# Linformer attention and a maxout feed-forward on one core: V projections through a doubled F, and one K/V projection moved by a slot

## The chip, the cores and the metric

The kernel runs on one core of a Trainium2 chip. The metric is the device time of one execution in microseconds, as a median of several runs. PE is the matrix engine (PEld its weight loads), DVE the vector engine, ACT the scalar engine, POOL the GpSimd engine and SP the queue of the sync engine.

## The reference

There are 8 batches of 8 heads, with 1024 positions and a head size of 64; E and F map the 1024 positions to 64.

```python
k_proj = np.einsum('ks,bhsd->bhkd', E, k)
v_proj = np.einsum('ks,bhsd->bhkd', F, v)
scores = (1 / np.sqrt(64)) * np.matmul(q, k_proj.transpose(0, 1, 3, 2))
attn = softmax(scores, axis=-1)
a = np.matmul(attn, v_proj)                    # (8, 8, 1024, 64)
x = a.transpose(0, 2, 1, 3).reshape(8192, 512)
h = np.maximum(np.maximum(x @ w1, x @ w2), x @ w3)   # 768 wide
out = h @ w_out                                # (8192, 512)
```

## The kernel before

The work is a pipeline over batches. While the feed-forward of batch b runs on PE, the attention of batch b+1 is laid between its groups of matmuls. A batch has two chunks of 512 rows. A chunk's layer 1 is 18 groups (`l1`, L212: six column tiles by three weights, four matmuls of 128x512 each, L215), and its down projection is four row blocks (`down`, L224, six matmuls each, L240). Layer 1 and down share a ring of four PSUM banks; the attention uses banks 4 to 7.

The order is written by hand. In the main loop every group of `l1` and every `down` ends a slot (`tick`, L560), and `at(slot, f, ...)` (L501) names what is emitted after which slot. Each engine executes its instructions in the order in which they are emitted. For batch 1 the list stands at L504 to L518: the K/V projection `kv` (L120) at slot 22, four Q transposes on DVE (`q_flip`, L103), the loads of batch 2 (`load_behind_turn`, L91) behind the transposed K projection, scores from slot 28 on. `kv` uses 16 matmuls (E on K at L123, F on V at L125, into the two halves of bank 4), two casts on ACT, two copies on DVE and a DMA transpose on SP's queue (L133) into `kpT`, which the scores (L145) read.

Batch 0 has its own opening, before the loop, since nothing is there yet that could hide its loads. E and F are loaded, cast and transposed by PE into `eT` and `fT` (L394 to L402; ACT evicts F). The loads of K, V and w1 to w3 and half of Q are issued from POOL, L370 to L384; the loads of w_out (L467) and those of batch 1 (L468 to L470) follow on the same queue. K and V of batch 0 are projected in pairs of heads. `v_proj0(g, bank)` (L282) takes 8 slices of 128 positions; for each it issues two matmuls with a 128x64 slice of F as weights and 64 columns of one head of V, one for each half of the output partitions; one DVE copy (L287) takes 128x64 into `vp2`. `half(g, u)` (L263) says which partitions a head of a pair gets: it swaps them for odd pairs. Between the steps stand warm-up matmuls (`warmup`, L350) on zeroes, that feed nothing.

The part around the change is emitted as follows: the projections of pairs 0 and 1, `av0(., 0)` (the products of probabilities and V for heads 0 to 3, L463), their normalisation on DVE (`norm0`, L309), the projection of pair 2 into bank 3 (L481), one warm-up matmul, the first slice of w1 over six column tiles (`w1_ct(0)`, L445, which writes bank 3 last), the projection of pair 3 into bank 7 (L484), three tiles of the second slice, then `av0(., 1)` for heads 4 to 7, and the remaining slices of w1.

In the last chunk of the kernel (c = 15), `down` (L226) splits row blocks 2 and 3 into two halves of 256 columns each, evicted by DVE and ACT and written out from the queues of SP and ACT. The other row blocks are evicted by ACT as a whole.

Of the kernel before, what the change touches and what calls it, by code (L numbers as in the profile page):

```python
# [10 lines left out]
BF16 = mybir.dt.bfloat16  # L11
# [5 lines left out]
def kernel(ctx: ExitStack, tc: tile.TileContext, q, k, v, E, F, w1, w2, w3, w_out, out):  # L17
    nc = tc.nc
    B, H, S, D = q.shape
    KP = E.shape[0]  # L20
    P = 128
    SI = S // P
# [9 lines left out]
    def T(shape, dt, name):  # L32
        return sb.tile(shape, dt, name=name)

    ps = pp.tile([P, 8, 512], FP32, name="ps")
# [5 lines left out]
    sel = T([P, 4, P], BF16, "sel")  # L41
    kp_0 = T([P, 2, 2, NPAIR, KP], BF16, "kp_0")
    eT = T([P, SI, KP], BF16, "eT")
    fT = T([P, SI, KP], BF16, "fT")
    w_sb = [T([P, NCT, DF], BF16, f"w{i}_sb") for i in range(3)]
    wo_sb = T([P, NJT, DO], BF16, "wo_sb")

# [2 lines left out]
    v_t = [T([P, H, SI, D], BF16, f"v_t{i}") for i in range(NB)]  # L50
# [4 lines left out]
    vp2 = [T([P, NPAIR, 2, D // 2], BF16, f"vp2_{i}") for i in range(3)]  # L55
# [5 lines left out]
    h1s = [T([P, 512], FP32, f"h1s{i}") for i in range(2)]  # L61
# [53 lines left out]
    HEAD = (0, 1, 2, 3, 5, 4, 7, 6)  # L115
# [107 lines left out]

    def down(b, ch, c, tt):  # L224
        o = o_acc[c % 2]
        if c == 2 * B - 1 and tt > 1:  # L226

            n = DO // 2
            for x in range(2):
                tmp = h1s[x] if tt == 3 else o[:, 2, x * n:(x + 1) * n]  # L230
                bank = fbank()
                for jt in range(NJT):
                    nc.tensor.matmul(out=ps[:, bank, :n], lhsT=hT[c % 2][:, jt, tt * P:(tt + 1) * P],  # L233
                                     rhs=wo_sb[:, jt, x * n:(x + 1) * n], start=(jt == 0), stop=(jt == NJT - 1))
                (nc.scalar.copy if x else nc.vector.tensor_copy)(out=tmp[:, :n], in_=ps[:, bank, :n])
                (nc.scalar if x else nc.sync).dma_start(out=out_v[b, ch][:, tt, x * n:(x + 1) * n], in_=tmp[:, :n])
            return
        bank = fbank()
        for jt in range(NJT):
            nc.tensor.matmul(out=ps[:, bank, :], lhsT=hT[c % 2][:, jt, tt * P:(tt + 1) * P],  # L240
                             rhs=wo_sb[:, jt, :], start=(jt == 0), stop=(jt == NJT - 1))
        nc.scalar.copy(out=o[:, tt, :], in_=ps[:, bank, :])  # L242
        if c == 2 * B - 1:
            nc.sync.dma_start(out=out_v[b, ch][:, tt, :], in_=o[:, tt, :])
        elif tt % 2 == 1:
            dst = out_v[b, ch] if b else out_0[ch]
            put = lambda: nc.gpsimd.dma_start(out=dst[:, tt - 1:tt + 1, :], in_=o[:, tt - 1:tt + 1, :])  # L247
            held.append(put) if c == 1 else put()
# [14 lines left out]
    def half(g, u):  # L263
        x = u ^ (g % 2)
        return slice(x * KP, (x + 1) * KP)
# [16 lines left out]
    def v_proj0(g, bank):  # L282
        for si in range(SI):
            for u in range(2):
                nc.tensor.matmul(out=ps[half(g, u), bank, g * D:(g + 1) * D], lhsT=fT[:, si, :],
                                 rhs=v_t[0][:, HEAD[2 * g + u], si, :], start=(si == 0), stop=(si == SI - 1))
        nc.vector.tensor_copy(out=vp2[0][:, g], in_=ps[:, bank, g * D:(g + 1) * D].rearrange("p (dd f) -> p f dd", f=2))  # L287

    def scores0(ch, g, bank):
        for u in range(2):  # L290
# [59 lines left out]
    def warmup(n, bank):  # L350
        for _ in range(n):
            nc.tensor.matmul(out=ps[:, bank, :], lhsT=warm[:, 0:P], rhs=warm, start=True, stop=True)
# [25 lines left out]
    for wt, w in zip(w_sb[1:], (w2, w3)):  # L378
        for hh in range(2):
            if wt is w_sb[2] and hh:  # L380
                nc.gpsimd.dma_start(out=q_1[:, 0:4], in_=qv_[1][:, 0:4])
            nc.gpsimd.dma_start(out=wt[:, 2 * hh:2 * hh + 2, :],
                                in_=w[hh * 256:(hh + 1) * 256].rearrange("(r f) n -> r f n", f=2))
# [10 lines left out]
    for y, dst in enumerate((eT, fT)):  # L394
        for si in range(SI):
            for x in range(2):
                nc.tensor.matmul(out=ps[x * D:(x + 1) * D, y, si * KP:(si + 1) * KP], lhsT=ef_b[:, y, si::SI],
                                 rhs=ident[:, x::2], start=True, stop=True)
        if y:
            for g in (0, 1):  # L400
                nc.scalar.copy(out=q_0[:, :, 2 * g, :], in_=q_st[:, HEAD[2 * g]])
        (nc.scalar.copy if y else nc.vector.tensor_copy)(out=dst.rearrange("p si k -> p (si k)"), in_=ps[:, y, :])  # L402

    def q_turn0(g):
        for n in range(4):
# [4 lines left out]
    def q_cast0(g):  # L410
        if g > 1:
            nc.scalar.copy(out=q_0[:, :, 2 * g, :], in_=q_st[:, HEAD[2 * g]])
        nc.vector.tensor_copy(out=q_0[:, :, 2 * g + 1, :], in_=q_st[:, HEAD[2 * g + 1]])

    SB = (0, 1, 4, 5)
    for g in range(NPAIR):
        q_cast0(g)
    warmup(1, 3)
    q_turn0(0)
    q_turn0(1)  # L420
# [57 lines left out]
    av0(1, 0)  # L478
    norm0(0, 0, 6, (0,))
    norm0(0, 1, 7, (0,))  # L480
    v_proj0(2, 3)  # L481
    warmup(1, 2)
    w1_ct(0)
    v_proj0(3, 7)  # L484
    w1_ct(1, range(3))
    av0(0, 1)
    av0(1, 1)
# [9 lines left out]
    for b in range(B):  # L497
        n = b + 1
        groups = []

        def at(slot, f, *args):  # L501
            groups.append((slot, lambda: f(*args)))

        if b == 0:  # L504
            at(8, q_up0, slice(4, 8))
            at(22, kv, 1)
            at(24, load_behind_turn, 2, "kvq")
            for g, x in enumerate((23, 24, 26, 27)):
                at(x, q_flip, 1, g)
            at(28, scores, 1, 0)  # L510
            at(31, scores, 1, 1)
            at(34, sums, 1)
            at(34, log, 1)
            at(34, recip, 0)
            at(35, recip, 1)
            at(36, av3, 1)
            at(37, norm, 1, 1, 0, AB)
            at(38, norm, 1, 0, 1, AB + 2)  # L518
        elif b == 1:
            at(2, kv, 2)  # L520
            for g in range(4):
                at(4 + g, q_flip, 2, g)
            at(9, load_behind_turn, 3, "kvq")
            at(10, scores, 2, 0)
            at(13, scores, 2, 1)
            at(16, sums, 2, 1)
            at(16, log, 1)
            at(17, recip, 0)
            at(19, recip, 1)
            at(24, load, 4, k, k_t)  # L530
            at(24, load, 4, v, v_t)
            at(25, av3, 2)
            at(26, norm, 2, 1, 0, AB)
            at(28, norm, 2, 0, 1, AB + 2)
            at(30, kv, 3)
            for g in range(4):
                at(32 + 2 * g, q_flip, 3, g)
        elif n < B:
            if b + 2 < B:
                at(3, lambda: kv(b + 2, fbank()))  # L540
            at(3, scores, n, 0)
            at(8, scores, n, 1)
            if b + 3 < B:
                at(11, load_behind_turn, b + 3, "qkv", 4 if b == 2 else None)
            at(14, sums, n, b)
            at(14, log, 1)
            at(15, recip, 0)
            at(17, recip, 1)
            at(26, av3, n)
            at(27, norm, n, 1, 0, AB)  # L550
            at(29, norm, n, 0, 1, AB + 2)
            if b + 2 < B:
                for g in range(4):
                    at(33 + 2 * g, q_flip, b + 2, g)
        else:
            at(5, av1, b)
        slot = 0
        gi = 0

        def tick():  # L560
            nonlocal slot, gi
            slot += 1
            while gi < len(groups) and groups[gi][0] <= slot:
                groups[gi][1]()
                gi += 1

        for ch in range(2):
            c = 2 * b + ch
            if c == 0:
                for part in ((1, range(6), (6, 7, 0, 1, 4, 5)), (2, range(3), (2, 3, 0), lambda: q_up0(slice(0, 4))),  # L570
                             (2, range(3, 6), (1, 2, 3), scores_up0)):
                    for _ in l1_first(*part):
                        tick()
                ring[:] = [0, 1, 2, 3]
                for x in range(2):
                    if x:
                        av_up0()
                    for tt in range(4):
                        down_half(tt, x)
                        if x:  # L580
                            tick()
                        elif tt == 0:
                            sums0(1, 4)
                continue
            for s in range(18):
                l1(b, ch, c, s // 3, s % 3)
                tick()
                if pend and s in (2, 5, 8, 11):
                    pend.pop(0)()
                    tick()  # L590
            pend = [lambda tt=tt, b=b, ch=ch, c=c: down(b, ch, c, tt) for tt in range(4)]
        if b == 0:
            while pend:
                pend.pop(0)()
                tick()
# [32 lines left out]
```

## Time and profile before

| | |
|---|---|
| median of 3 runs | 395.44 us (395.0 to 395.99) |
| the profiled execution | 394.96 us |
| its span, from the first to the last instruction | 393.1 us |
| PE busy | 387.7 us of the span |
| DVE, ACT, POOL busy | 202.5, 162.1, 67.0 us |
| DMA over the span | 123 GB/s mean; 205 GB/s in most of the first 50 us |

Times below are from the start of the span. A line of a timeline gives the start and the length of a run of like instructions, then engine, line, operation, tiles and count. Square brackets hold the idle time of the engine before it and what ended that.

### The profile page before, as it was taken

The page shows a single profiled execution, that of the slowest core. Times are in us where ns is not written, and L with a number is a line of the kernel's source. Part 1 is how long each engine was busy: PE and PEld are TensorE (multiplying, and loading weights), DVE is VectorE, ACT ScalarE, POOL GpSimd, SP SyncE. Part 2 cuts the span into 40 slices and gives each one's busy share as a digit, 9 for nine tenths or more (in the row PEclk, how much of TensorE's full clock was granted, in tenths as well). Part 3 has the DMA queues.
Part 4 walks back from the last instruction along what each step waited for, and adds up shares of the span by engine and source line. Part 5 has one row for each costly group of instructions (what it writes and reads, how often), then busy time and mean ns, then how long its engine had stood idle before and what let it go on. Part 6 is the DMA issues. An engine that isn't in the chain of part 4 may idle for free.

```text
span 393.1 us, 6707 instructions
## 1 busy us (share of the span) xinstructions
PE 387.7 (99%) x2768; PEld 173.2 (44%) x2768; DVE 202.5 (52%) x303; ACT 162.1 (41%) x248; POOL 67.0 (17%) x110
## 2 busy tenths in 40 slices
PE   8999999999999999999999999999999999999996
PEld 4444444444444444444444444444444444444443
DVE  3447565755663566345753357524664446453342
ACT  4413347374326622454224732266134542222221
POOL 7442132062004300050000600000010000000000
PEclk9999999999999999999999999999999999999999
DMA  8999989899974995169511992131011111111023
GB/s 221 206 210 204 205 173 203 135 208 206 206 160 86 201 205 179 24 123 206 157 53 28 172 212 101 53 82 53 2 58 50 54 55 54 55 45 63 0 106 107
DMA packets 41453, 48.39 MB, mean 123 GB/s; under 512 B 9168, under 2 KB 36560, under 8 KB 41424
## 3 DMA queue, kind: packets, MB, share of 16 engines
q0 software_dynamic: 31792, 43.52, 54.1%
q1 hardware_dynamic: 8656, 3.41, 4.8%
q10 hardware_dynamic: 976, 1.05, 0.8%
q8 instruction: 21, 0.34, 0.3%
q14 instruction: 8, 0.07, 0.0%
HBM read 57.15 MB, written 16.78 MB: 188 GB/s over the span
## 4 chain that ended last, share of the span: by engine, by line
PE 92%; DMA 6%; ACT 1%; POOL 0%; issue 0%; POOLq 0%
PE ps L215 59%; PE ps L240 19%; PE ps L123 3%; PE ps L159 3%; DMA w_sb<-in_moe_w_dram 3%; PE ps L456 2%; PE ps L145 2%; DMA k_t<-in_k_dram 2%; PE ps L254 1%; DMA kpT<-kp 1%; PE ps L447 1%; PE ps L233 1%; ACT pT L339 1%; PE ps L272 0%; POOL k_t L367 0%
## 5 line engine op out<-in xcount | busy, mean ns | idle before, releaser
L215 PE MATMUL ps<-xT,w_sb 128*128 128x512 bf16 x1080 | 244.3, 379 | 0.0
L215 PEld LDWEIGHTS <-w_sb 128*128 128x128 bf16 x1080 | 103.8, 98 | 129.7 <-issue 8.0
L220 DVE TENSOR_TENSOR m<-ps,h1s 128x512 f32<-128x512 f32 x90 | 62.0, 689 | 131.5 <-PE ps L215 98.4
L240 PE MATMUL ps<-wo_sb,hT 128*128 128x512 bf16 x348 | 84.2, 379 | 0.0
L218 ACT COPY h1s<-ps 128x512 f32<-128x512 f32 x90 | 52.9, 588 | 71.9 <-PE ps L215 71.7
L242 ACT COPY o_acc<-ps 128x512 f32<-128x512 f32 x58 | 34.0, 586 | 99.9 <-PE ps L240 99.9
L222 DVE TENSOR_TENSOR hT<-ps,m 128x512 bf16<-128x512 f32 x90 | 62.0, 689 | 8.1
L247 POOL DMA_DIRECT2D out_dram<-o_acc x28 | 15.2, 542 | 253.4 <-ACT o_acc L242 246.6
L240 PEld LDWEIGHTS <-hT 128*128 128x128 bf16 x348 | 33.4, 98 | 41.5 <-issue 2.3
L179 DVE TENSOR_TENSOR xT<-ps,rinv 128x1024 bf16<-128x1024 f32 x28 | 33.4, 1217 | 11.2 <-PE ps L159 11.2
L150 ACT ACTIVATE pT<-ps 128x1024 bf16<-128x1024 f32 x28 | 27.1, 1021 | 5.3 <-PE ps L145 4.9
L105 DVE STREAM_TRANSPOSE qT<-q_t 128x512 f32<-128x512 f32 x28 | 18.5, 686 | 0.0
L89 POOL DMA_DIRECT2D v_t<-in_v_dram x21 | 15.3, 753 | 8.4 <-PE ps L215 3.0
L170 ACT ACTIVATE lns<-ps 128x1024 f32<-128x1024 f32 x14 | 13.6, 1023 | 3.9 <-PE ps L159 3.9
L173 ACT ACTIVATE rinv<-lns 128x1024 f32<-128x1024 f32 x14 | 14.9, 1061 | 0.0
L125 PE MATMUL ps<-v_t,fT 128*64 128x512 bf16 x56 | 13.4, 382 | 0.0
L123 PE MATMUL ps<-k_t,eT 128*64 128x512 bf16 x56 | 13.4, 382 | 0.0
L129 ACT CAST kp<-ps 64x512 bf16<-64x512 f32 x7 | 4.0, 578 | 18.5 <-PE ps L125 18.5
L89 POOL DMA_DIRECT2D k_t<-in_k_dram x14 | 10.6, 770 | 5.8 <-DMA k_t<-in_k_dram 2.3
L89 POOL DMA_DIRECT2D q_t<-in_q_dram x14 | 10.6, 779 | 1.5 <-DMA wo_sb<-in_moe_w_out_dram 1.1
L456 PE MATMUL ps<-xT,w_sb 128*128 128x512 bf16 x48 | 10.9, 379 | 0.0
L131 DVE COPY kp<-kp 64x1536 bf16<-64x1536 bf16 x7 | 3.9, 552 | 12.8 <-ACT kp L129 12.8
(88 smaller groups left out, 166.0 us busy)
## 6 DMA issues: line engine op xcount, KB each, us to landing
out_dram<-o_acc POOLq DMA_DIRECT2D x30, 512.0 KB, 2.9
k_t<-in_k_dram POOLq DMA_DIRECT2D x14, 512.0 KB, 12.7
q_t<-in_q_dram POOLq DMA_DIRECT2D x14, 512.0 KB, 12.2
v_t<-in_v_dram POOLq DMA_DIRECT2D x18, 256.0 KB, 15.2
v_t<-in_v_dram POOLq DMA_DIRECT2D x7, 512.0 KB, 14.9
w_sb<-in_moe_w_dram POOLq DMA_DIRECT2D x4, 384.0 KB, 10.3
k_t<-in_k_dram POOLq DMA_DIRECT2D x4, 256.0 KB, 8.0
w_sb<-in_moe_w_dram POOLq DMA_DIRECT2D x4, 192.0 KB, 9.7
```

The source lines that it names most:

```text
L89: nc.gpsimd.dma_start(out=dst[b % NB][:, slots], in_=sv[:, heads])
L105: nc.vector.transpose(out=qT[b % NB][:, hs].bitcast(FP32).rearrange("p h n -> p (h n)"), in_=q_t[b % NB][:, hs].rearrange("p h si d -> p ( ...
L123: nc.tensor.matmul(out=ps[0:KP, bank, :], lhsT=eT[:, si, :], rhs=k_t[i][:, :, si, :], start=(si == 0), stop=(si == SI - 1))
L150: nc.scalar.activation(out=pT[i][:, 2 * u + gg].rearrange("p ch (t r n) -> p r (ch t) n", t=4, r=4), in_=ps[:, AB:AB + 4, gg * 256:(gg + 1 ...
L179: nc.vector.tensor_tensor(out=xT[b % 2][:, f::2, ch, :], in0=ps[:, bank:bank + 2, :], in1=rinv[ch].rearrange("p (u n) -> p u n", u=2), op= ...
L215: nc.tensor.matmul(out=ps[:, bank, :], lhsT=w_sb[i][:, ct, jt * P:(jt + 1) * P], rhs=xT[b % 2][:, ct, ch, :], start=(ct == 0), stop=(ct == ...
L218: nc.scalar.copy(out=h1s[jt % 2], in_=ps[:, bank, :])
L220: nc.vector.tensor_tensor(out=m12[jt % 2], in0=ps[:, bank, :], in1=h1s[jt % 2], op=ALU.max)
L222: nc.vector.tensor_tensor(out=hT[c % 2][:, jt, :], in0=ps[:, bank, :], in1=m12[jt % 2], op=ALU.max)
L240: nc.tensor.matmul(out=ps[:, bank, :], lhsT=hT[c % 2][:, jt, tt * P:(tt + 1) * P], rhs=wo_sb[:, jt, :], start=(jt == 0), stop=(jt == NJT - 1))
L242: nc.scalar.copy(out=o[:, tt, :], in_=ps[:, bank, :])
L456: nc.tensor.matmul(out=ps[:, bank, :], lhsT=w_sb[i][:, ct, jt * P:(jt + 1) * P], rhs=xT[0][:, ct, 0, :], start=(ct == 0), stop=(ct == NCT ...
```

## The change

F is kept twice side by side: `fT2` has two copies of each 128x64 slice, and `fT` becomes a view of the first. A copy on POOL, emitted after the casts of Q and before the first Q transposes of batch 0, fills the second. The V projections of pairs 2 and 3 of batch 0 use a new function, `v_wide0`: for each slice one matmul with both copies as 128x128 weights and two heads of V as 128 columns. Of its output, a quarter for each head is kept, by two DVE copies of 64x64. The K/V projection of batch 1 is emitted after slot 21 in place of 22. In the last chunk only row block 3 is split in halves; row block 2 goes the way of the others.

```diff
-    fT = T([P, SI, KP], BF16, "fT")
+    fT2 = T([P, SI, 2, KP], BF16, "fT2")
+    fT = fT2[:, :, 0, :]
...
-        if c == 2 * B - 1 and tt > 1:
+        if c == 2 * B - 1 and tt == 3:
 
             n = DO // 2
-            for x in range(2):
-                tmp = h1s[x] if tt == 3 else o[:, 2, x * n:(x + 1) * n]
+            for x, tmp in enumerate(h1s):
...
+    def v_wide0(g, bank):
+        for si in range(SI):
+            nc.tensor.matmul(out=ps[:, bank, 0:2 * D], lhsT=fT2[:, si].rearrange("p x k -> p (x k)"),
+                             rhs=v_t[0][:, 2 * g:2 * g + 2, si, :], start=(si == 0), stop=(si == SI - 1))
+        for x in range(2):
+            slot = HEAD[2 * g + x] - 2 * g
+            nc.vector.tensor_copy(out=vp2[0][half(g, x), g],
+                                  in_=ps[half(g, x), bank, slot * D:(slot + 1) * D].rearrange("p (dd f) -> p f dd", f=2))
+
...
-        (nc.scalar.copy if y else nc.vector.tensor_copy)(out=dst.rearrange("p si k -> p (si k)"), in_=ps[:, y, :])
+        (nc.scalar.copy if y else nc.vector.tensor_copy)(out=dst, in_=ps[:, y, :].rearrange("p (si k) -> p si k", k=KP))
...
     for g in range(NPAIR):
         q_cast0(g)
+    nc.gpsimd.tensor_copy(out=fT2[:, :, 1, :], in_=fT)
     warmup(1, 3)
...
-    v_proj0(2, 3)
+    v_wide0(2, 3)
     warmup(1, 2)
     w1_ct(0)
-    v_proj0(3, 7)
+    v_wide0(3, 7)
     w1_ct(1, range(3))
...
-            at(22, kv, 1)
+            at(21, kv, 1)
```

## The prediction

> **What bounds the kernel now.** I read the busy shares first, then the chain of waits in order of time, then the timelines of PE and POOL around the edit.
>
> ```profile
> PE 387.7 (99%) x2768; PEld 173.2 (44%) x2768; DVE 202.5 (52%) x303; ACT 162.1 (41%) x248; POOL 67.0 (17%) x110
> ```
>
> PE is idle for 393.1 - 387.7 = 5.4 us in the whole span, so a gain has little room, while a new wait of PE is paid almost in full. The chain of waits shows the two places where PE is released by something other than itself near the edit:
>
> ```profile
> 10.28 9.85 DMA w_sb<-in_moe_w_dram
> 20.13 0.05 issue
> 20.18 0.82 PE ps L447 x3
> ...
> 51.03 4.39 DMA kpT<-kp
> 55.41 0.04 issue
> 55.46 0.66 PE ps L145 x29
> ```
>
> At 20.18 the second slice of w1 has just landed; from there the chain is PE work, until the scores of batch 1 wait for the transposed K projection (landed near 55.42). Between the two projections of the edit PE is full (columns: start, us, engine, line, operation):
>
> ```profile
> 16.98 0.68 PE L272 MATMUL ps<-pT,vp 64*32 64x512 bf16 x8
> 17.59 0.44 PE L285 MATMUL ps<-v_t,fT 128*64 128x64 bf16 x16
> 17.96 0.39 PE L352 MATMUL ps<-warm 128*128 128x512 bf16 x1
> 18.30 1.46 PE L447 MATMUL ps<-xT,w_sb 128*128 128x512 bf16 x6
> 19.68 0.44 PE L285 MATMUL ps<-v_t,fT 128*64 128x64 bf16 x16
> 20.18 0.82 PE L447 MATMUL ps<-xT,w_sb 128*128 128x512 bf16 x3
> ```
>
> The timeline of POOL over the same stretch decides the case:
>
> ```profile
> 18.14 0.75 POOL L381 DMA_DIRECT2D q_t<-in_q_dram  x1 [0.43 <-DMA w_sb<-in_moe_w_dram]
> 19.48 0.53 POOL L382 DMA_DIRECT2D w_sb<-in_moe_w_dram  x1 [0.59 <-DMA v_t<-in_v_dram]
> 20.41 0.75 POOL L384 DMA_DIRECT2D q_t<-in_q_dram  x1 [0.40 <-DMA w_sb<-in_moe_w_dram]
> 21.33 0.75 POOL L467 DMA_DIRECT2D wo_sb<-in_moe_w_out_dram  x1 [0.17 <-issue]
> ```
>
> POOL issues the loads in program order (its q load of L381 sits between two weight loads of L382, as written), and each late one waits until an earlier load has landed: L384 starts at 20.41, 0.3 us after the w1 slice landed at 20.13. The new copy is written after L384 and before L467, so it inherits that time.
>
> [...] So nothing behind a waiting projection can fill PE. The trace agrees in that all its matmuls appear in program order. [...] nine matmuls of 512 columns take 4.02 us there, 0.43 us each, against 0.216 later (six of L447 in 1.46 us: (1.46 - 0.379) / 5). [...] six matmuls from 18.30 would end their turn at 18.30 + 6 x 0.216 = 19.60, and the 128x64 projection starts at 19.68.
>
> **The change, part by part.**
>
> Second copy of F. One POOL copy of 128x512 bf16, not in the trace. Its start: L384 ends at 20.41 + 0.75 = 21.16, and the idle before L467 is 0.17, so 21.3. Its length: POOL's smallest copy (128x1) takes 0.19 us; [...] No run shows it. [...] I take 0.62: end 21.92. VectorE norm to PE took 0.1 (norm starts at 17.55, ends near 18.2, PE at 18.30), so PE may go on at T = 22.03 (21.8 to 22.7).
>
> The wait that it adds. The projection of pair 2 reads both copies of F. It stood at 17.59; now PE stands until T. Behind it on PE are the warm-up matmul, the whole of w1's first slice, the projection of pair 3, and everything after. ACT and DVE have only work that comes from PE: nothing fills in. The two projections before it and the K/V projection of batch 1 read only the first copy. Strided neighbours are not taken for overlaps: the Q transposes of L406 ran from 7.46, while a cast of L412 into interleaved columns of the same tile, earlier in the program, started at 8.27.
>
> Wide projections. Eight matmuls of 128 columns with 128x128 weights, for sixteen of 64. Starts of the old ones are (0.44 - 0.196) / 15 = 16 ns apart, so its two halves overlap: there is no idle half to win. The nearest row for the new form, the transposes of L406 (eight in 0.61 us, 0.219 each), gives (0.61 - 0.219) / 7 = 56 ns. From start to next operation: old 0.37 (16.29 to 16.66) plus 0.08 for the mode change = 0.45; new 0.44 (7.46 to 7.90), no change of mode between the wide ones. Zero either way, 0.1 as bound.
>
> From T then: wide 0.45, warm-up 0.22, w1 slice 6 x 0.216 = 1.30, wide 0.45; w1's second slice at T + 2.42, without a wait for its weights, landed at 20.13. It was at 20.18, so PE is late by 22.03 + 2.42 - 20.18 = **4.27 us**. I carry it to the end: after 20.18 PE is its own releaser but for the one wait below.
>
> Evictions. Two copies of 64x64 for one of 128x64, which took 0.22; half the partitions save nothing, so +0.22 for each pair on DVE. Pair 2: bank 3 is written again by the sixth w1 matmul, 1.75 after T, and the copies are done by T + 1.1. Pair 3: done 0.61 + 0.05 + 0.44 = 1.1 after its start, and the V product that needs it comes 0.45 + 0.75 = 1.2 after. Hidden by 0.1 only; without that cover up to 0.2.
>
> POOL's later loads. L467 is pushed from 21.33 to about 22.1; the second to 23.0, ending by 23.8. The next load (24.73) waits for a landing near 24.1. Cost zero; the loads in flight hide it. PE is then 4.27 us later against its loads, so none becomes late.
>
> K/V of batch 1 a slot earlier. It moves ahead of one layer-1 group: four matmuls, 0.86 us, and one DVE maximum. It brings sixteen matmuls, two ACT casts, two DVE copies (0.55 + 0.42), one transpose on SP's queue; SP and POOL issue nothing in between that it passes. Its last V load was issued at 31.51 and took 14.9, landing at 46.4; even unshifted, 47.85 - 0.86 = 46.99 is after that. The maximum behind the two DVE copies is up to 0.8 us later; its bank is needed again 2.6 us after. Removed: PE's wait before the scores, 0.40 us (55.06 to 55.46). What is late next there: nothing, as the transpose lands 5.7 us after the projection's end and seven groups take 6.05. The batch's last Q load (34.44 + 17.0 = 51.4) no longer competes either. **-0.40**.
>
> The tail. The third row block of the last chunk is again one full down projection: six matmuls of 512 (1.30) for twelve of 256 (24 in 2.63, so 1.32): -0.02. Its ACT copy (0.58) ends near 388.9 and its one transfer of 256 KB follows the two halves issued at 388.07 and 388.68 before. The last half-transfers (389.45, 389.99, landing 1.8 later) may share bandwidth with it: 0 to 0.3, taken 0.1.
>
> F's cast into strided rows (ACT, 0.58) has 0.39 us of idle behind it: nothing.
>
> **Sum**: 4.27 - 0.40 - 0.02 + 0.10 = +3.95. The profiled execution took 394.96 (span 393.1 and 1.86 around it), so 398.9; that run is 0.48 under the median of 395.44, and against the median I forecast **399.4**.
>
> **Rivals.** *The array goes cold too.* PE is idle from about 17.66 to 22.03, 4.4 us. [...] The loss: at most the opening's 4.02 - 9 x 0.216 = 2.1[...]; I take 1.7: 401.1. *Not slower: the copy runs early.* F is ready at 7.87 and POOL is idle for 2.0 us before 9.19; were the copy to run in that hole, ending before 17.5, PE would not wait and only -0.40 + 0.08 stays: 395.1. It decides at a copy end of about 17.5. Against it: POOL keeps written order everywhere. *The copy holds up all readers of F.* If the first copy's readers wait too, PE stops at 14.29: 22.03 - 14.29 = 7.74, less 0.3, plus 1.7 cold: 404.5. The strided casts above speak against it.
>
> **Numbers.** Stall alone 0.52, own range 398.9 to 400.3[...]; stall and cold array 0.36; copy early 0.08; all readers 0.04. Range 398.6 to 401.8: it leaves out the last two and the end of the cold case. About 0.3%, 1.2 us, is what a measurement can tell from no change: faster 0.02, same 0.06, slower 0.92.
>
> **What would show it.** PE idle from 17.6 to near 22.0, released by the POOL copy, which follows L384; L447 matmuls at 0.43 us each after it if cold; two wide projections of about 0.6 us; no wait before the scores of batch 1. It is wrong if the copy stands before 17 us, or if PE fills the gap.

## The result and the profile after

The changed kernel takes 400.78 us in the median of 4 runs (400.32 to 400.99), against 395.22 of the kernel before. The ratio is 1.0137, with a 95% interval of 1.0118 to 1.0156: 5.56 us slower. The forecast was 399.4 with a range of 398.6 to 401.8. The range held, but what happened is not the likeliest case: it is the rival in which the array goes cold as well (the granted clock of PE is 0.50 from 22.55 to 25.96), worked out as 401.1. The profiled execution took 400.62 us, with a span of 398.7.

First the busy shares of the kernel after. The kernel before has 2768 matmuls and 2768 weight loads; with 16 fewer in the wide projections and 6 fewer in the tail PE should have 2746 of both here. 51 records of matmuls are missing, so PE's busy time is understated.

```profile
PE 385.7 (97%) x2695; PEld 173.3 (43%) x2746; DVE 202.7 (51%) x304; ACT 162.5 (41%) x248; POOL 67.6 (17%) x111
```

The chain of waits of the kernel after, in order of time (start, us, what):

```profile
10.16 10.36 DMA w_sb<-in_moe_w_dram
20.51 0.28 issue
20.80 0.75 POOL q_t L393
21.55 0.63 POOL fT L427
22.18 0.05 issue
22.23 0.77 PE ps L291 x8
23.00 0.43 PE ps L361
23.42 2.56 PE ps L457 x6
25.98 0.50 PE ps L291 x8
```

In the kernel before, the landing of w1's second slice released PE. Now the same landing releases POOL's load of L393; POOL's copy comes behind that, and only then PE. POOL in the kernel after:

```profile
20.80 0.75 POOL L393 DMA_DIRECT2D q_t<-in_q_dram  x1 [0.41 <-DMA w_sb<-in_moe_w_dram]
21.54 0.63 POOL L427 COPY fT<-fT 128x512 bf16<-128x512 bf16 x1
```

The timeline of PE in the kernel after shows the hole and what follows it:

```profile
16.88 0.68 PE L272 MATMUL ps<-pT,vp 64*32 64x512 bf16 x8
22.23 0.77 PE L291 MATMUL ps<-v_t,fT 128*128 128x128 bf16 x8 [4.67 <-POOL fT L427]
22.79 0.63 PE L361 MATMUL ps<-warm 128*128 128x512 bf16 x1
23.22 2.77 PE L457 MATMUL ps<-xT,w_sb 128*128 128x512 bf16 x6
25.78 0.70 PE L291 MATMUL ps<-v_t,fT 128*128 128x128 bf16 x8
...
27.06 0.61 PE L272 MATMUL ps<-pT,vp 64*32 64x512 bf16 x8
```

The six matmuls of L457 take 2.77 us where the same six took 1.46. The busy time by stretch of the kernel after tells why; the third number from the right of a line is the granted clock of PE:

```profile
17.60:22.00 4.40, 0.00 (x0) 0.00 (x0) 1.14 (x2) 0.00 (x0) 3.00 (x5) 1.00 1.17 212
22.00:24.00 2.00, 1.77 (x11) 1.01 (x12) 0.45 (x2) 0.00 (x0) 1.62 (x3) 0.64 1.09 214
24.00:26.00 2.00, 2.00 (x8) 0.81 (x7) 0.00 (x0) 0.00 (x0) 0.78 (x1) 0.51 1.06 207
26.00:28.00 2.00, 1.95 (x20) 0.84 (x20) 0.87 (x3) 0.00 (x0) 0.74 (x1) 1.00 1.32 206
```

No matmul from 17.6 to 22.0, then a granted clock of 0.64 and 0.51 up to 26, then 1.00. How late PE is can be read at two places, the V products of heads 4 to 7 and the first row block of the last down projection. In the kernel before:

```profile
20.93 0.61 PE L272 MATMUL ps<-pT,vp 64*32 64x512 bf16 x8
...
384.18 2.75 PE L240 MATMUL ps<-wo_sb,hT 128*128 128x512 bf16 x12
```

In the kernel after:

```profile
389.83 4.05 PE L240 MATMUL ps<-wo_sb,hT 128*128 128x512 bf16 x18
```

The V products begin at 27.06 in place of 20.93: 6.13 late. At the last down projection PE is 389.83 - 384.18 = 5.65 late, and the span is 5.6 longer. So the loss is made before 27 us, and some 0.5 of it comes back later.

### The profile page after: what moved, and what is told of

Same layout as the page of the kernel before. It is cut to its first block, busy times and chain, and to the rows that moved or that the text cites. A ratio compares the mean times of both kernels' runs of the same rounds, so it can differ in the third digit from the quotient of the medians.

```text
span 398.7 us, 6611 instructions
## 1 busy us (share of the span) xinstructions
PE 385.7 (97%) x2695; PEld 173.3 (43%) x2746; DVE 202.7 (51%) x304; ACT 162.5 (41%) x248; POOL 67.6 (17%) x111
## 4 chain that ended last, share of the span: by engine, by line
PE 92%; DMA 4%; issue 1%; POOL 1%; ACT 1%; POOLq 0%
PE ps L216 59%; PE ps L240 19%; PE ps L124 3%; PE ps L160 3%; DMA w_sb<-in_moe_w_dram 3%; PE ps L466 2%; PE ps L146 2%; DMA k_t<-in_k_dram 2%; PE ps L457 2%; PE ps L254 1%; ACT pT L348 1%; PE ps L272 0%; PE ps L233 0%; PE ps L291 0%; POOL k_t L376 0%
## 5 line engine op out<-in xcount | busy, mean ns | idle before, releaser
L130 ACT CAST kp<-ps 64x512 bf16<-64x512 f32 x7 | 4.1, 579 | 17.6 <-PE ps L126 17.6
```

## The experiments

Theory: two losses in a row, the wait for POOL's copy because of its place behind the loads, and the half clock after the idle stretch. Rivals: the wide form itself is dear; the copy disturbs the loads; the lateness comes from elsewhere. The kernel before was run beside each group again: 395.0, 394.94 and 394.93 in the median.

**The copy on DVE.**

```diff
-    nc.gpsimd.tensor_copy(out=fT2[:, :, 1, :], in_=fT)
+    nc.vector.tensor_copy(out=fT2[:, :, 1, :], in_=fT)
```

> The second copy of F is made by DVE in place of POOL; all else as in the changed kernel. Theory (the loss is the wait for POOL's place behind the loads, and the cold array after it): no idle time before the wide projection of pair 2, no half-rate matmuls after it, and what is left is the scores' wait and the tail, 0.4 to 0.55 below the kernel before: 394.7 to 394.9. Rival (the wide form itself is dear, through its full-array weights or its two evictions): the time stays over 396, although PE no longer waits for POOL.

Measured: 395.11, ratio 0.9999 (0.9991 to 1.0007). The loss is gone, with both wide projections in place. PE in this kernel:

```profile
17.41 0.62 PE L291 MATMUL ps<-v_t,fT 128*128 128x128 bf16 x8
17.87 0.38 PE L361 MATMUL ps<-warm 128*128 128x512 bf16 x1
18.17 1.47 PE L457 MATMUL ps<-xT,w_sb 128*128 128x512 bf16 x6
19.49 0.61 PE L291 MATMUL ps<-v_t,fT 128*128 128x128 bf16 x8
20.66 0.59 PE L457 MATMUL ps<-xT,w_sb 128*128 128x512 bf16 x2 [0.56 <-DMA w_sb<-in_moe_w_dram]
```

No hole, 1.47 us for the slice; PE waits for w1's second slice, as before the change. But the 0.4 that were to be gained by K/V's move don't show.

**The narrow form with POOL's copy left in.** Nobody reads the second copy of F.

```diff
-    v_wide0(2, 3)
+    v_proj0(2, 3)
...
-    v_wide0(3, 7)
+    v_proj0(3, 7)
```

> The POOL copy stays where it is, but pairs 2 and 3 are projected in the old narrow form, so nobody reads the second copy. Theory: POOL's copy costs nothing by itself, 394.7 to 394.9. Rival (the copy delays the loads behind it on POOL, and these come late): above 396, with idle time of PE before the down projection of the first chunk or before the K/V projection of batch 1.

Measured: 394.99, ratio 0.9997 (0.9989 to 1.0005). POOL's copy costs nothing when nobody waits for it. Wide (the run above) and narrow differ by 0.12 us, less than a measurement can tell.

**The wait filled.**

```diff
+    warmup(20, 2)
     v_wide0(2, 3)
```

> Twenty warm-up matmuls of 512 columns (4.3 us) are put before the wide projection of pair 2, so that PE is busy while POOL gets to its copy; the wait stays. Theory (two terms, 4.45 of waiting and 1.66 of half rate): the six matmuls of the first w1 slice go at 0.216 each, and the time is 1.6 to 1.7 below the changed kernel, near 399.1. Rival (the slow stretch after the wait belongs to the wide form or to something else than the idle time): no gain, 400.6 to 401.

Measured: 399.16, ratio 1.0101 (1.0086 to 1.0115), 1.62 below the changed kernel. The dummy matmuls stand where PE was idle, and the mean granted clock of the profiled execution is 1.0, against 0.995 in the changed kernel:

```profile
18.81 4.49 PE L361 MATMUL ps<-warm 128*128 128x512 bf16 x20
23.14 0.61 PE L291 MATMUL ps<-v_t,fT 128*128 128x128 bf16 x8
23.80 1.46 PE L457 MATMUL ps<-xT,w_sb 128*128 128x512 bf16 x6
```

(The opening of this execution ran 1.3 us late, which the lengths don't feel. POOL's copy ended at 21.76, before the dummy matmuls did, so this trace doesn't show the wait itself; its time, 399.98, is the longest of the four.) So 1.6 of the 5.6 us are the half clock. That the rest is the wait follows from the runs without it.

**The copy two loads earlier on POOL.** The load loop of w2, w3 and the second half of Q (L387 to L393) is emitted where the copy stood, with the copy inside it. Between this place and the old one stand two loads, the last of w3 and the last of Q; the expectations count three.

```diff
...
             if wt is w_sb[2] and hh:
                 nc.gpsimd.dma_start(out=q_1[:, 0:4], in_=qv_[1][:, 0:4])
+            if wt is w_sb[2] and hh:
+                nc.gpsimd.tensor_copy(out=fT2[:, :, 1, :], in_=fT)
...
```

> POOL's copy is put three loads earlier in its queue, between the first half of the second Q load and the last load of w3. By the trace of the changed kernel it can start near 19.3, so PE may go on at 20.0: idle for 2.4 us in place of 4.7. Theory (PE follows the place of the copy one to one[...]): w1's second slice starts at 20.0 + 2.42 = 22.4, 2.2 later than in the kernel before, so 395.2 + 2.2 - 0.5 = 396.9. Rival (any idle stretch of microseconds costs the half-rate time as well): 398.6. Rival (the place in the queue doesn't matter): 400.8.

Measured: 398.06, ratio 1.0065 (1.0048 to 1.0081), but in two groups: 396.64 and 396.84 with a mean granted clock of 0.999, and 397.9 to 398.38 (four executions) with 0.994 to 0.996. The lower group is the theory's 396.9, the upper one the rival's 398.6, less a little. The profile was of the lower group:

```profile
20.05 0.62 PE L291 MATMUL ps<-v_t,fT 128*128 128x128 bf16 x8 [2.50 <-POOL fT L425]
20.50 0.38 PE L361 MATMUL ps<-warm 128*128 128x512 bf16 x1
20.72 1.46 PE L458 MATMUL ps<-xT,w_sb 128*128 128x512 bf16 x6
```

The copy runs two loads sooner, from 19.36 in place of 21.54, and PE goes on at once: the place sets the wait.

**The same once more.** No edit.

> The kernel with POOL's copy three loads earlier once more; its executions fell into two groups, near 396.7 and near 398.2, and the profile was of the first, with a warm array. Theory (an idle stretch of 2.5 us leaves the array cold in some executions): a profile near 398.2 shows the first w1 slice at 0.43 us a matmul and a granted clock near 0.5 after the wait. Rival (a load lands late in those executions): the matmuls go at 0.216 and the 1.5 us stand as idle time elsewhere.

Measured: 398.37 (clock 0.995) and 396.79 (0.999). This time the profile is of the upper group:

```profile
19.75 0.62 PE L291 MATMUL ps<-v_t,fT 128*128 128x128 bf16 x8 [2.21 <-POOL fT L425]
20.21 0.58 PE L361 MATMUL ps<-warm 128*128 128x512 bf16 x1
20.58 2.77 PE L458 MATMUL ps<-xT,w_sb 128*128 128x512 bf16 x6
```

An idle stretch of 2.21 us was followed by the half clock, one of 2.50 us in the other execution was not. In the slow one the time goes into the matmuls, not into a wait for a load: the loads are out as a cause.

**K/V a slot earlier, alone**, on the kernel before.

```diff
-            at(22, kv, 1)
+            at(21, kv, 1)
```

> The kernel before, with the K/V projection of batch 1 at slot 21 as its only edit. Theory (moving it takes away the scores' wait of 0.40 to 0.48; what cancels it in the two kernels with no wait for POOL is a w1 slice that lands 0.3 to 0.45 later, which comes with the doubled F): 394.5 to 394.6. Rival (the wait's end is not worth its length, something later takes it back): 395.0.

Measured: 395.05, ratio 1.0004 (0.9996 to 1.0012). No gain: the theory fell here.

**The doubled tile alone**, on the kernel before (the tile and the view of it, and the cast of F into strided rows; no copy, no wide form).

```diff
-    fT = T([P, SI, KP], BF16, "fT")
+    fT2 = T([P, SI, 2, KP], BF16, "fT2")
+    fT = fT2[:, :, 0, :]
...
```

> The kernel before, with only F's tile doubled, so that F's cast writes strided rows and later tiles move in memory; nobody fills or reads the second copy. Theory (the later landing of the w1 slice comes with the doubled F): 395.3 to 395.45, the slice lands at 20.4 to 20.6. Rival (the landing differs from run to run and the kernel before was profiled in an early one): 395.0.

Measured: 394.96, ratio 1.0003 (0.9995 to 1.0011). The doubled tile costs nothing; a later landing of the w1 slice isn't its doing.

**The kernel before, a second profile.** No edit.

> The kernel before once more, for a second profile of it. If the landing of w1's second slice at 20.13 belongs to this kernel, it lands there again within 0.1; if it varies from run to run, it may land at 20.4 to 20.6, and the scores' wait should then be seen at the same length.

Measured: 394.98. Its lines at the w1 slice and at the scores:

```profile
20.55 0.59 PE L447 MATMUL ps<-xT,w_sb 128*128 128x512 bf16 x2 [0.27 <-DMA w_sb<-in_moe_w_dram]
...
55.46 0.66 PE L145 MATMUL ps<-qT,kpT 32*64 32x256 bf16 x32 [0.26 <-DMA kpT<-kp]
```

The slice came later than in the first profile, and the V products behind it began at 21.07 in place of 20.93; yet the scores begin at 55.46 in both. The wait there is slack: 0.40 in one execution, 0.26 in the other. The transpose in the kernel with the narrow form, K/V at slot 21, shows what holds it:

```profile
L134 SPq DMA_TRANSPOSE kpT<-kp x1: 1317/1317/1317, 50.6 to 50.6; - x1
...
DMA to landing us min/median/max: 4.9/4.9/4.9
```

Issued at 50.6 it lands near 55.5. In the kernel before it was issued at 51.03 and landed at 55.42. With the copy on DVE: 50.42 and 55.1; with K/V moved alone: 51.2 (a late opening) and 55.3. So an issue that is 0.4 or 0.6 us earlier brought a landing between 0.1 later and 0.3 earlier. With the copy on DVE the scores did begin 0.2 earlier in the profiled execution, at 55.24, but the medians show no gain. What else is under way are the last Q load (landing at 51.4 in the kernel before) and the two output stores of L259 (landing at 52.7 and 54.5).

**The copy on POOL, ahead of the later loads**: the same load loop is emitted behind the copy.

```diff
+    nc.gpsimd.tensor_copy(out=fT2[:, :, 1, :], in_=fT)
     for wt, w in zip(w_sb[1:], (w2, w3)):
...
```

> POOL's copy stays on POOL, but stands before the loads of w2, w3 and the second half of Q, so it can start near 13.3. Theory (it is the place in the queue that costs, not the engine): no wait before the wide projection of pair 2, the loads behind the copy keep their times since they wait for landings anyway, and the time is that of the kernel before, 394.9 to 395.2. Rival (a copy on POOL amid the loads delays these): 395.5 or more, with later landings of w2 and w3.

Measured: 395.02, ratio 1.0002 (0.9994 to 1.001). The copy runs from 13.46 to 14.08, the next load is issued at 14.25 (14.12 in the kernel before), and PE has no wait for POOL. Same engine, same copy, another place: no loss.

**The changed kernel with K/V back at slot 22.**

```diff
-            at(21, kv, 1)
+            at(22, kv, 1)
```

> The changed kernel with the K/V projection of batch 1 back at slot 22. Theory (the scores' wait of the kernel before hangs on when the load queue is through with batch 1, which is a fixed time; six microseconds later nothing is left of it, at either slot): no wait before the scores, 400.3 to 401, as the changed kernel. Rival (the slot is worth its 0.4 there too): 401.1 to 401.4, with the wait at the scores.

Measured: 401.16 (399.98 to 401.72), ratio 1.0161 (1.0147 to 1.0175), which overlaps the changed kernel's interval: by the time alone inconclusive. The trace decides: its V products of heads 4 to 7 are 26.39 - 20.93 = 5.46 late, its last down projection 389.17 - 384.18 = 4.99, so 0.47 come back, as in the changed kernel (0.48); the transpose lands in 3.6 us, issued at 56.49, before PE is through with the groups ahead of the scores. So late, the scores' wait is gone at either slot. The spread is in the clock: mean 0.994 in the shortest execution, 0.991 in the other four.

**Shorter idle stretches.** Six warm-up matmuls in the kernel with the copy two loads earlier, then ten in the changed kernel.

```diff
+    warmup(6, 2)
     v_wide0(2, 3)
```

> The kernel with POOL's copy three loads earlier, with six warm-up matmuls of 512 columns before the wide projection of pair 2, so that PE idles for about 1.1 us in place of 2.2 to 2.5. Theory (the group near 398.2 is the cold array, and needs an idle stretch of some 2 us): all executions in the group near 396.7. Rival (the second group comes from the loads): still some near 398.2.

Measured: 396.76, ratio 1.0043 (1.0031 to 1.0056); all five between 395.97 and 397.05, clocks 0.999 to 1.0. The upper group is gone. In the profiled one the opening was late and nothing was left idle.

```diff
+    warmup(10, 2)
     v_wide0(2, 3)
```

> The changed kernel with ten warm-up matmuls in place of twenty: PE is busy until about 19.4 and then idle for 2.5 to 2.8 us up to the copy's end. Theory (what counts is the length of the idle stretch, and 2.2 to 2.5 us were enough in some executions): a mixture of executions near 399.2 and near 400.8. Rival ([...]): all near 399.2.

Measured: 400.62, ratio 1.0128 (1.0108 to 1.0148), in two groups again: 398.88 and 399.0 with clocks of 1.0, 400.62 to 400.88 (three) with 0.995 to 0.996. The mixture came as the theory has it. The profile is of the lower group; its opening was late too, so PE idled less than foreseen:

```profile
22.16 0.62 PE L291 MATMUL ps<-v_t,fT 128*128 128x128 bf16 x8 [1.86 <-POOL fT L427]
```

How long the other four idled isn't recorded.

## Why the prediction was right, and where it was off

**The wait for POOL.** Right in its cause and nearly in its size. The copy was forecast from 21.3 to 21.92 and ran from 21.54 to 22.17; its 0.63 us come close to the 0.62, which was an estimate of mine that no trace had shown, as was the range from 21.8 to 22.7 for PE; its start is later because the w1 slice landed at 20.51 and not at 20.13. PE went on at 22.23, for 22.03. Nothing behind the waiting projection ran on PE before that: the warm-up matmul of L361, which reads neither copy, starts at 22.79. With the forecast's 2.42 to w1's second slice the wait is 22.23 + 2.42 - 20.18 = 4.47 us, for 4.27. Three runs confirm it: copy on DVE or early on POOL, no loss; two loads earlier, about 1.6 to 1.9 in the group with the clock up. Where the copy was moved in the program, it moved on POOL: it starts at 13.46, 19.36 and 21.54 in the three places. Readers of the first copy weren't held up: the projection of pair 1 starts at 16.18 (16.29 before).

**The cold array.** This is the step that failed, in its chance: the 0.36 was an estimate of mine that no trace had shown, and so the likeliest case and the 399.4 were wrong. The traces show when the clock changes. In the changed kernel it rises at 5.48, falls at 22.55, rises at 25.96 and falls at 398.01, after PE's last work; between these lie 5, 1 and 109 times 3.413 us. In the kernel before it rises at 6.47 and falls at 392.18, 113 times as long. In all fourteen traces kept, every change of the granted clock on record comes a whole multiple of 3.413 us (from 1 to 115 times) after the change before it, and each of the three cold stretches after the wait that were profiled lasts 3.41 us, from 22.55 to 25.96 in the changed kernel, from 21.29 to 24.70 with K/V at slot 22, from 20.25 to 23.67 in the second profile with the copy two loads earlier. I call each stretch of 3.413 us between two such times a window. Below, the time around the wait is cut at the borders of these windows; where the clock didn't fall, they are counted on from its first rise in the opening. The number after the comma is PE's busy time, the third from the right the clock. First the changed kernel:

```profile
19.13:22.55 3.42, 0.32 (x6) 0.33 (x7) 0.00 (x0) 0.00 (x0) 2.46 (x5) 1.00 1.13 211
22.55:25.96 3.41, 3.41 (x15) 1.45 (x13) 0.45 (x2) 0.00 (x0) 1.85 (x3) 0.50 1.09 214
```

The copy two loads earlier, second profile (idle for 2.21 us):

```profile
16.84:20.25 3.41, 1.20 (x18) 0.68 (x18) 1.32 (x3) 0.01 (x1) 2.37 (x4) 1.00 1.19 207
20.25:23.67 3.42, 3.42 (x15) 1.50 (x13) 0.44 (x2) 0.00 (x0) 2.27 (x3) 0.50 1.11 215
```

The same kernel, first profile (idle for 2.50 us):

```profile
15.22:18.64 3.42, 2.17 (x31) 0.82 (x28) 2.55 (x5) 1.62 (x3) 1.07 (x3) 1.00 1.21 207
18.64:22.05 3.41, 2.00 (x16) 1.18 (x17) 0.54 (x3) 0.00 (x0) 2.83 (x5) 1.00 1.14 211
22.05:25.46 3.41, 3.36 (x27) 1.52 (x27) 1.73 (x4) 0.00 (x0) 1.83 (x3) 1.00 1.10 218
```

Ten dummy matmuls (idle for 1.86 us):

```profile
19.39:22.80 3.41, 1.55 (x14) 0.76 (x12) 0.00 (x0) 0.00 (x0) 2.59 (x5) 1.00 1.13 213
22.80:26.22 3.42, 3.42 (x28) 1.56 (x27) 1.28 (x5) 0.00 (x0) 1.53 (x2) 1.00 1.09 215
```

The 2.21 us lay in one window, and the clock was 0.50 in the next. The 2.50 us were split by a border and left no window with more than 1.41 us of idle time, and the clock stayed at 1.00. So the clock fell at the border of a window that was not wholly idle: 2.21 us of idle PE in one of 3.41 were enough, 1.86 were not. A stretch of 4.4 us leaves some window with at least 4.4 / 2 = 2.2 us of idle time wherever the borders fall, so by this estimate from the 2.21 us the cold array was close to certain. The limit rests on five profiled executions; that all four runs of the changed kernel have a mean clock of 0.991 to 0.995, and all five of its variant with slot 22 as well, fits it. The price was right for one cold window: 1.7 estimated; 6.13 - 4.47 = 1.66 in the trace, 1.62 by filling the wait.

**The wide projections.** Right: nothing gained, nothing lost. With the copy on DVE, from the start of the first to the next operation 0.46 (0.44 forecast), and the second takes over 0.02 after its turn where the narrow one, the only one of the two whose tile changes (`128*128` to `128*64`, the forecast's mode change), needed 0.08. The two evictions take 0.46 us for 0.22 and stay hidden.

**The scores' wait.** The number came out nearly right, by luck: 0.40 was forecast as the gain of the earlier slot, and 0.48 came back in the changed kernel, but 0.47 came back with K/V at slot 22 too. The gain belongs to PE's lateness and not to the slot: the transpose is issued at 56.3 and lands in 3.6 us, before PE gets to the scores at 61.12. Without the stall the slot gained nothing that the medians show. The rival without the stall was put at 395.1, and the copy early on POOL and the copy on DVE took 395.02 and 395.11; but 395.1 was 0.3 under the 395.44 of the kernel before as it stood then, and beside these runs that kernel took 394.93 and 395.0. In the kernel before the 0.40 was one execution's slack, 0.26 in another, and the reasoning that seven groups of 6.05 us cover the 5.7 of the transpose overlooked that the earlier transpose took longer to land: 4.7 and 4.9 us, for 4.4 and 4.2. That the Q load and the stores hold it is argued from their landing times, not shown by a run; nor is a gain of 0.1 to 0.2 excluded.

**POOL's later loads and the tail.** Right. The first two loads of batch 1 are issued at 24.81 and 26.73 (24.73 and 26.51 before), late by the same 0.1 to 0.2 as landings are there. From the last down projection's start to the span's end it is 8.9 us in both kernels, with spans that are given to 0.1; +0.08 had been forecast, and no run changes the tail alone.

**The sum.** 4.47 + 1.66 - 0.48 = 5.65, the lateness at the last down projection, and 5.6 is the difference of the spans. It closes by the way its terms were taken, as differences of times in the same two traces; what supports the split is that filling the wait gave back 1.62, and moving the copy on POOL gave back all of it.

## What to carry to other kernels

A small operation put on the engine that issues the loads takes its place in that queue, and with it the landings that the loads ahead of it wait for: here PE idled for 4.67 us behind a copy of 0.63 us, for 2.2 and 2.5 us with the copy two loads earlier, and it had no wait for POOL with the copy ahead of the loads. Look up when the queue reaches that line, not when the operand is ready. Price a stall of the matrix engine with the slow clock after it (1.66 us here), as soon as some 2 us of idleness can fall into one window of 3.41 us: 2.21 us brought the clock down, 1.86 us didn't. A filler of dummy matmuls bought that part back (1.62 us) but not the stall. A wait that ends on a transfer's landing need not be worth its length in one profile: the 0.40 us were 0.26 in another, and taking them away by itself brought no gain (395.05, against 394.94). Take a second profile before counting it as gain.

## What the runs showed that was not expected

The clock falls after shorter idle stretches than I had thought, and not every time. In the two kernels without a filler where PE idled for 4.2 and 4.7 us in the profiled executions it fell in nine of nine. With the copy two loads earlier, where two profiles show 2.2 and 2.5 us, it fell in five of eight; the idle times of the executions that weren't profiled are not on record. In these two profiles the borders of the windows decided: at 2.2 us all of it lay in one window, at 2.5 us no window had more than 1.41. The mean granted clock of an execution tells which it was (0.991 to 0.996 against 0.998 to 1.0). One cold window takes 3.41 / 2 / 398.7 = 0.004 off that mean, so executions at 0.991 may have had two, an estimate, as no such execution was profiled; the two of the changed kernel took 0.5 us longer than its other two. In the opening the busy time by stretch reads 1.00, though matmuls take 0.43 us each: the record of the clock begins with its first rise, at 5.48 in the changed kernel. And a 64x64 eviction on DVE takes as long as a 128x64 one: 222 ns on average.
